# Joining the first loads to the list of steps, moving four x adds to GpSimd, and re-interleaving a tuned kernel

## The chip, the cores and the metric

The kernel runs on one core of a Trainium2 chip. The metric is the time of one execution in microseconds (us), measured on the device; each kernel is executed several times and the median is quoted. The profile's "span" is a little shorter than this time: it runs from the first to the last recorded piece of work. Each execution also gives the mean clock that TensorE was granted (1.0 is full, 0.5 is half).

## The reference

Linear attention over 8 batches, 8 heads, 576 positions and 64 features a head, followed by a gated layer over 4608 tokens of 512 features.

```python
q_s = softmax(q, axis=-1)                 # over the 64 features
k_s = softmax(k, axis=2)                  # over the 576 positions
kv  = einsum('bhsd,bhse->bhde', k_s, v)   # "key-value product"
x   = einsum('bhsd,bhde->bhse', q_s, kv)  # then laid out as (4608, 512)
H   = maximum(x @ w_h, 0)
T   = 1 / (1 + exp(-(x @ w_t + b_t)))
out = T * H + (1 - T) * x
```

## The kernel before

Each engine works through its own list in order, as the traces show: in the kernel before, the scale of batch 1's last q block starts at 32.28 us, behind a cast that waited for its data until 31.65. The kernel is a set of small step functions and one long list `order` that says in which order they are issued, so the list is the schedule of all engines. A step's name tells its engine: `exp_half` and `tanh` run on ScalarE; `q_sums`, `kv_norm`, `diff` and `blend` on VectorE; `q_scale_p`, `cast_v` and `add_x` on GpSimd; `kv_half`, `q_trans`, `x_pair`, `gate` and `carry` on TensorE. The parts that the change and the argument touch:

```python
def q_scale_p(b, n0, n1):                 # GpSimd: q exponentials times 1/sum
    e, r = eq[b][:, n0:n1], qsum[b][:, n0:n1]
    nc.gpsimd.tensor_mul(e, e, r.broadcast_to(list(e.shape)))

def gate(c, ob, ps=None):                 # TensorE: x @ w_t, four 128x512 matmuls ("pt")
    ...
def carry(c, ob):                         # TensorE: x @ (w_h - 1), the same shape ("ph")
    ...

# which 128-wide blocks of x are added on GpSimd, by pair of batches; TensorE adds the others
added = lambda g: ((0, 1), (0, 1), (0, 1), (0, 1, 2, 3))[g]

def add_x(c, ob):
    xv, gv = views(c)
    eng = nc.vector if (c, ob) == (B - 1, 3) else nc.gpsimd
    eng.tensor_add(gv(ob), gv(ob), xv(ob))

def turn_block(t, k_, xs, us):            # TensorE: turn a block to rows ("nat"), add x on the way
    dst = t[:, k_, :]
    if xs is not None:
        mm(dst, xs, ident, True, False)   # one more matmul where GpSimd has not added x
    mm(dst, us, ident, xs is None, True)

def warm_up(n):                           # TensorE: matmuls whose result nobody reads;
    for _ in range(n):                    # put in to keep the clock up (measured under a_fill)
        mm(warm, ident, wide, True, True)
```

q of batches 6 and 7 is turned by a DMA (`q_turn`, the tile `qsD`) instead of by TensorE. The loads of batches 0 and 1 and of the weights stand in front of the list, before any step.

The softmax here doesn't subtract the row's maximum and nothing guards it: scores larger than these inputs give would overflow.

## Time and profile before

| | before |
|---|---|
| time, median (lowest to highest of the first runs) | 129.05 us (128.37 to 129.15) |
| time, span and mean clock of the profiled run | 130.35 us (a slow run, over 1.5% above the fastest), 127.4 us, 0.962 |
| TensorE, VectorE, ScalarE, GpSimd busy | 88%, 76%, 73%, 59% |
| first gate group of batch 0 / key-value product of batch 1 / first gate group of batch 1 | 18.1 / 28.5 / 33.2 us |
| last row tile of the output starts (its last wait is on VectorE) | 123.2 us |

The page divides the span into 40 slices of 3.18 us; a digit is the busy share in tenths, and the PEclk row gives TensorE's clock in tenths of full. The lines themselves are shown in the prediction. Two groups matter for the adds: the x adds on GpSimd and the matmuls that turn blocks to rows. The columns are line, engine, operation, tiles, count, then busy us and mean ns of one, then the idle time before them. The first line is of the page, the second of the full list of groups (`--lines`); it holds the matmuls that add x:

```profile
L428 POOL TENSOR_TENSOR g<-g,xT 128x512 f16<-128x512 f16 x19 | 21.7, 1153 | 10.3 <-DVE g L417 9.5
...
L64 PE MATMUL nat<-ident,xT 128*128 128x128 f16 x48 | 7.9, 219 | 0.0
```

### The profile page before, as it was taken

The numbers are of one execution on the slowest core, as the hardware profiler recorded it, in microseconds if no ns is written. First come the engines' busy times: TensorE is split into PE (matmuls) and PEld (weight loads), VectorE is DVE, ScalarE is ACT, GpSimd is POOL, SyncE is SP. The second block draws the span as 40 slices with busy tenths as digits, with TensorE's granted clock in tenths as the row PEclk, the third lists the DMA queues.
The fourth block names the chain that finished last, engine by engine and source line by source line (L and its number), as shares of the span: only waits on it lengthen the run. The fifth ranks groups of instructions, "written<-read, shape, count | busy, mean of one in ns | idle before, by whom it ended". The sixth has DMA issues, their size and how long they took to land.

```text
span 127.4 us, 3361 instructions
## 1 busy us (share of the span) xinstructions
PE 111.8 (88%) x1375; PEld 62.1 (49%) x1375; DVE 96.2 (76%) x179; ACT 93.0 (73%) x130; POOL 75.0 (59%) x71
## 2 busy tenths in 40 slices
PE   4996599584699998999999998999999999999940
PEld 2343334252224643654564466555555555599820
DVE  1089548399938899899799997879975649799960
ACT  4156076995694879768997989999999794576740
POOL 2004524960679393996991697499797224855510
PEclk9999999999558999999999999999999999999995
DMA  3999999999999999999999999948517816007994
GB/s 127 349 377 388 404 404 408 413 410 413 403 413 410 413 400 413 410 406 408 418 412 412 404 412 413 390 108 226 211 26 141 342 49 291 5 39 332 422 380 150
DMA packets 20583, 41.24 MB, mean 324 GB/s; under 512 B 5460, under 2 KB 5976, under 8 KB 19544
## 3 DMA queue, kind: packets, MB, share of 16 engines
q1 hardware_dynamic: 20568, 41.03, 84.4%
q8 instruction: 10, 0.16, 0.5%
q14 instruction: 5, 0.04, 0.1%
HBM read 30.41 MB, written 9.44 MB: 313 GB/s over the span
## 4 chain that ended last, share of the span: by engine, by line
PE 54%; DMA 20%; DVE 11%; SPq 4%; ACT 4%; issue 2%; POOL 2%; DVEq 1%; POOLq 1%
PE ph L64 20%; PE pt L64 20%; DMA v<-in_v_dram 10%; DMA w32h<-in_moe_w_h_dram 10%; PE nat L64 7%; SPq L94 4%; DVE g L417 3%; PE pq L69 3%; PE px L64 2%; DVE r L228 2%; ACT pt L396 1%; DVE qsT L278 1%; PE psk L64 1%; DVE dd L409 1%; DVE kvn L217 1%
## 5 line engine op out<-in xcount | busy, mean ns | idle before, releaser
L258 POOL TENSOR_TENSOR eq<-eq,r 128x1024 f16<-128x1024 f16 (+2 forms) x16 | 29.7, 1878 | 12.0 <-DVE r L246 9.7
L64 PE MATMUL ph<-xT,w16h 128*128 128x512 f16 x128 | 33.7, 389 | 2.2 <-ACT w16h L114 1.6
L64 PE MATMUL pt<-xT,w16t 128*128 128x512 f16 x128 | 33.6, 395 | 0.0
L396 ACT ACTIVATE pt<-pt,bt 128x512 f32<-128x512 f32 (+1 forms) x40 | 24.5, 622 | 8.8 <-PE pt L64 8.6
L409 DVE SCALAR_TENSOR_TENSOR dd<-xT,ph 128x512 f16<-128x512 f16 x32 | 21.5, 678 | 10.9 <-PE ph L64 9.8
L428 POOL TENSOR_TENSOR g<-g,xT 128x512 f16<-128x512 f16 x19 | 21.7, 1153 | 10.3 <-DVE g L417 9.5
L417 DVE SCALAR_TENSOR_TENSOR g<-pt,dd 128x512 f16<-128x512 f32 (+1 forms) x40 | 24.7, 627 | 2.3 <-ACT pt L396 1.1
L178 ACT ACTIVATE eq<-q 128x1152 f16<-128x1152 f32 x16 | 18.4, 1165 | 5.7 <-DMA q<-in_q_dram 5.7
L64 PEld LDWEIGHTS <-w16t 128*128 128x128 f16 x160 | 15.1, 100 | 13.8 <-issue 2.8
L64 PEld LDWEIGHTS <-w16h 128*128 128x128 f16 x160 | 14.4, 99 | 14.7 <-issue 2.5
L178 ACT ACTIVATE ek<-k 128x1152 f16<-128x1152 f32 x16 | 18.7, 1172 | 1.8 <-DMA k<-in_k_dram 1.8
L228 DVE TENSOR_REDUCE r<-eq 128x18 f32<-128x1152 f16 x12 | 16.0, 1344 | 5.2 <-ACT eq L178 5.2
L468 ACT COPY o<-nat 128x512 f32<-128x512 f32 x28 | 16.6, 592 | 4.5 <-PE nat L64 4.0
L189 POOL CAST v<-v 128x1152 f16<-128x1152 f32 x12 | 13.9, 1184 | 9.8 <-DMA v<-in_v_dram 9.8
L64 PE MATMUL nat<-ident,g 128*128 128x128 f16 x142 | 16.3, 220 | 0.1
L64 PEld LDWEIGHTS <-g 128*128 128x128 f16 x144 | 12.4, 98 | 6.5 <-DVE g L417 1.1
L64 PE MATMUL warm<-wide,ident 128*128 128x512 f16 x41 | 11.0, 423 | 1.8 <-DVE wide L149 1.8
L278 DVE COPY qsT<-pq 128x1024 f16<-128x1024 f16 (+1 forms) x18 | 9.9, 552 | 2.2 <-PE pq L69 2.0
L69 PE MATMUL pq<-ident,eq 128*128 128x128 f16 x108 | 8.9, 221 | 3.0 <-POOL eq L258 1.8
L361 ACT CAST xT<-px 128x1024 f16<-128x1024 f32 x10 | 10.2, 1018 | 1.8 <-PE px L64 1.5
L69 PEld LDWEIGHTS <-eq 128*128 128x128 f16 x108 | 6.9, 98 | 6.1 <-POOL eq L258 2.1
L64 PEld LDWEIGHTS <-ident 128*128 128x128 f16 x46 | 4.7, 105 | 7.6 <-issue 2.3
(53 smaller groups left out, 105.3 us busy)
## 6 DMA issues: line engine op xcount, KB each, us to landing
out_dram<-o SPq DMA_DIRECT2D x8, 1024.0 KB, 4.6
q<-in_q_dram SPq DMA_DIRECT2D x7, 1152.0 KB, 13.4
k<-in_k_dram SPq DMA_DIRECT2D x7, 1152.0 KB, 12.9
v<-in_v_dram SPq DMA_DIRECT2D x5, 1152.0 KB, 14.6
v<-in_v_dram SPq DMA_DIRECT2D x6, 576.0 KB, 12.0
q<-in_q_dram SPq DMA_DIRECT2D x2, 576.0 KB, 4.1
k<-in_k_dram SPq DMA_DIRECT2D x2, 576.0 KB, 7.0
w32t<-in_moe_w_t_dram SPq DMA_DIRECT2D x1, 1024.0 KB, 10.9
```

Of the source, the lines that this page charges most:

```text
L64: mm = lambda o, l, r, st, sp: nc.tensor.matmul(o, l, r, start=st, stop=sp, skip_group_check=True)
L69: nc.tensor.matmul(o, i, ident, is_transpose=True, start=True, stop=True, skip_group_check=True,)
L178: nc.scalar.activation(dst[b][:, :, 2 * a : 2 * a + 2, :], in32[which][b][:, 2 * a : 2 * a + 2].rearrange("p c n d -> p n c d"), AF.Exp,)
L189: nc.gpsimd.tensor_copy(o, i)
L228: nc.vector.reduce_sum(qsum[b][:, :, h], eq[b][:, :, h, :], axis=AX.X)
L258: nc.gpsimd.tensor_mul(e, e, r.broadcast_to(list(e.shape)))
L278: nc.vector.tensor_copy(qsT[b][:, :, n0:n1, :], turned_q.pop((b, g)))
L396: nc.scalar.activation(ps, ps, AF.Tanh, bias=bt2[:, ob : ob + 1], scale=0.5)
L409: nc.vector.scalar_tensor_tensor(dd, xv(ob), -0.5, ps, op0=ALU.mult, op1=ALU.max)
L417: nc.vector.scalar_tensor_tensor(gv(ob), th, 1.0, dd, op0=ALU.add, op1=ALU.mult)
L428: eng.tensor_add(gv(ob), gv(ob), xv(ob))
L468: copy(rows_of_four((g, n // 4))[:, n % 4, :], nat.pop((g, n)))
```

## The change

It has three parts. The first loads become steps of the list, in a new order. Pairs 1 and 2 (chunks 2 to 5) get their third block of x added on GpSimd, so that TensorE saves 16 matmuls. And the whole list is interleaved anew, with the aim of leaving TensorE no stretch so thin that its clock is lowered. The diff is 26 KB, nearly all of it the list; its core:

```diff
-    for w in "qkv":
-        load(0, w, 2)
-    nc.sync.dma_start(brow, moe_b_t.rearrange("(k p) -> k p", p=P))
-    load_weight("t", moe_w_t, "q32")
-    load(1, "q")
-    load_weight("h", moe_w_h, "k32", 4)
-    load(1, "k")
-    load(1, "v", 2)
+    def load_bias():
+        nc.sync.dma_start(brow, moe_b_t.rearrange("(k p) -> k p", p=P))
@@
-    added = lambda g: ((0, 1), (0, 1), (0, 1), (0, 1, 2, 3))[g]
+    added = lambda g: ((0, 1), (0, 1, 2), (0, 1, 2), (0, 1, 2, 3))[g]
@@  (the list; the stretch around batch 1's last q block, before)
-        ("exp_half", 2, "q", 0), ("blend", 0, 0), ("exp_half", 2, "q", 1), ("kv_norm", 1),
-        ("x_pair", 1, 0, False, ("ht", "ht")), ("blend", 0, 1), ("x_copy", 1, 0, "AV"),
-        ("cast_v_head", 2, 0, "P"), ("x_pair", 1, 1, False, ("ht", "q2")),
-        ("q_sums_tree", 2, 0), ("x_copy", 1, 1, "AV"), ("q_scale_p", 1, 8, 9),
-        ("q_trans", 1, 2), ("gate", 0, 3, "nat"), ("cast_v_head", 2, 3, "A"),
@@  (the list; its start, and the same stretch, after)
+        ("warm_up", 24), ("load", 0, "q", 2), ("exp_half", 0, "q", 0), ("load", 1, "q"),
+        ("load", 0, "v", 2), ("cast_v", 0, 1), ("warm_up", 6), ("exp_half", 0, "q", 1),
+        ("warm_up", 1), ("q_sums", 0, 1), ("load", 0, "k", 2), ("warm_up", 4),
+        ...
+        ("blend", 0, 0), ("kv_norm", 1), ("q_scale_p", 1, 8, 9), ("q_trans", 1, 2),
+        ("x_pair", 1, 0, False, ("ht", "ht")), ("tanh", 0, 3), ("exp_half", 2, "q", 0),
+        ("q_copy", 1, 2), ("blend", 0, 1), ("x_pair", 1, 1, False, ("ht", "q2")),
+        ("cast_v_head", 2, 2, "P"), ("x_copy", 1, 0, "AV"), ("x_copy", 1, 1, "AV"),
+        ("gate", 1, 1), ("exp_half", 2, "q", 1), ("add_x", 0, 0), ("carry", 1, 2),
+        ...
```

## The prediction

The phase is where the clock's windows of 3.41 us begin. "0.50 and 1.00 only" is the granted clock of the kernel before, and "there" in "1153 ns there" is GpSimd.

> **What bounds the kernel now.** I read the page first, then windows cut at the clock's own steps, then the timeline and the chain of waits around the first idle stretch. Parts 1 and 2 of the page:
>
> ```profile
> PE 111.8 (88%) x1375; PEld 62.1 (49%) x1375; DVE 96.2 (76%) x179; ACT 93.0 (73%) x130; POOL 75.0 (59%) x71
> ...
> PE   4996599584699998999999998999999999999940
> ...
> PEclk9999999999558999999999999999999999999995
> DMA  3999999999999999999999999948517816007994
> ```
>
> One slice is 127.4 / 40 = 3.18 us. TensorE (PE) is the fullest engine and is nearly solid from slice 12 to the end. Before that it has holes, and there the DMA row is solid: the first 30 us run at the pace of the loads, the rest at the pace of TensorE. Loads keep the DMA row full to slice 26 (83 us), but from 33 us no compute engine shows a wait on a load, so they run ahead. In slices 11 and 12 TensorE's granted clock is half. Windows of the clock's length, 3.41 us (columns: window, length, busy us and count of PE, PEld, DVE, ACT, POOL; then granted clock, DMA share, GB/s):
>
> ```profile
> 21.98:25.39 3.41, 1.85 (x11) 0.76 (x10) 1.50 (x5) 3.31 (x6) 3.20 (x4) 1.00 1.04 410
> 28.81:32.22 3.41, 1.43 (x78) 0.74 (x66) 3.34 (x8) 2.10 (x2) 0.57 (x1) 1.00 1.04 411
> 33.00:35.63 2.63, 2.62 (x8) 1.11 (x9) 2.53 (x7) 1.36 (x3) 1.06 (x1) 0.50 1.04 405
> 35.63:39.05 3.42, 3.42 (x16) 1.09 (x15) 0.95 (x2) 3.42 (x5) 3.29 (x3) 0.50 1.04 411
> 39.05:42.46 3.41, 3.41 (x57) 1.93 (x56) 2.90 (x7) 1.50 (x4) 2.75 (x3) 1.00 1.04 411
> ```
>
> TensorE was busy 42% of 28.81 to 32.22, and the clock halved at 32.22. It was busy 54% of 21.98 to 25.39, and nothing happened. After the drop came a window 77% busy (nothing from 32.22 to 33.00, then 2.62 of 3.41 us), which did not bring the clock back; the next, full one did, at 39.05. So 33.00 to 39.05, 6.05 us of dense matmuls, ran at half speed and lost 3.0 us. What emptied 28.81 to 32.22, from the chain of waits cut to 28 to 36 us and the timeline of ScalarE:
>
> ```profile
> 18.78 12.73 DMA v<-in_v_dram
> ...
> 31.65 0.67 POOL v L197
> 32.32 0.64 POOL eq L258
> ...
> 33.01 0.40 PE pq L69 x2
> ```
> ```profile
> 30.12 2.22 ACT L178 ACTIVATE eq<-q 128x1152 f16<-128x1152 f32 x2 [1.41 <-DMA q<-in_q_dram]
> ```
>
> GpSimd (POOL) stands in its in-order list on a cast of batch 2's v, which lands at 31.65; the scale of batch 1's last q block stands behind it, and TensorE's transposes behind that. ScalarE (ACT) meanwhile waits for batch 2's q (30.12) and does two exponentials before the copy that frees x of batch 1.
>
> [...] 0.50 and 1.00 only, steps 3.41 us apart; whether the phase moves the drop, one profile cannot show. [...] 128x512 adds take 1153 ns there against 880 ns for the single one on VectorE (DVE). [...] the trace moves 403 to 413 in most slices to 80 us. So reordering loads cannot bring the same bytes sooner, only other bytes first.
>
> **The change part by part.**
>
> *First loads.* Before: q0, k0, v0, bias, gate weights, q1, carry weights, k1, v1. After: q0, q1, v0, k0, bias, gate weights, carry weights, k1, v1. At 2.9 us per 1.18 MB tensor (1.18 MB / 0.408 MB per us), k0 goes from second to fourth place and lands near 15.6 us instead of 9.8; q1 lands near 9.8 instead of 18.1. The same bytes precede v1, so v1 lands near 27.3 in both (GpSimd waits for it until 27.31 before). Batch 0's first gate moves from 18.1 us to about 20.8: two exponentials at 1.15 us after k0, 72 small matmuls 0.8, normalise 0.7, x 0.8, copies 1.5, weight casts to 20.7. That costs nothing: before batch 1's key-value product (28.47 before) stand four gate groups and three carry groups in the new order, three and four in the old. Seven groups at 0.86 us (the chain's length for four 512-wide matmuls) plus transposes are 6.9 us, and 20.8 + 6.9 = 27.7. The new order fills this stretch with real work late instead of real work early and warm-up later; counts of warm-up matmuls are equal (41 + 5).
>
> *The idle stretch.* In the new order batch 1's last q block is scaled before any cast of batch 2's v, so the wait to 33.0 falls. What remains: ScalarE has one exponential of batch 2's q ahead of the x copies. q2 has the same bytes before it, so 30.1 + 1.15 + 2 copies at 0.6 = 32.45 for the next gate group against 33.09 (33.01 and two small transposes). Gain 0.6 us. From 29.1 to 32.45 TensorE has about 1.0 us of work, so the clock may well fall here again in spite of the change's aim. But then solid work starts at 32.45, the window 32.22 to 35.63 would be 93% busy (the initial window, 1.50 to 4.91, was 91% busy and released the clock), and one half-clock window instead of two would be spent: gain 1.4 us. If it does not fall at all: 3.0 us. I weigh them 60 to 40: 2.0 us.
>
> *x adds.* Pairs 1 and 2 (chunks 2 to 5) get their third block's x added on GpSimd: 4 more adds at 1.15 us = 4.6 us of GpSimd. Taken away: 8 row tiles x 2 pairs = 16 matmuls of 128x128 with their weight loads (TensorE's list goes from 2751 rows to 2719). A tile of six of these takes 0.34 us in the chain, 57 ns each: 16 x 57 = 0.9 us, on the engine that bounds.
>
> *The rest of the interleaving* changes no counts. TensorE idles some 1.3 us between 40 and 121 us before; I see as many new small holes as closed ones (a gap of some 0.9 us near 44 us, where ScalarE does batch 3's exponentials, landing 38.9, ahead of a tanh and two x copies). I put 0. From the start of the last gate's matmuls (120.69) to the end, 6.7 us: same parts in almost the same order, 0.
>
> Sum: 0.6 + 2.0 + 0.9 = 3.5 us, all after 30 us, where TensorE's list sets the pace, so it should reach the end: 129.05 - 3.5 = 125.5 us.
>
> **The rivals.**
> 1. *GpSimd becomes the bound late.* After batch 7's q scales come five adds in a row (5.8 us). Counting back from the new end, TensorE reaches the first row tile of pair 2 near 95.8 us; the scales can end near 89.8 (before: 91.97 + 4.19 = 96.2), so the fifth add ends near 95.6. That is level; a slip costs 1 to 2 us, making 127. For it: the adds also wait for blends. Against: GpSimd is only 59% busy.
> 2. *The clock was not the loss in the timed runs.* [...] if the three timed runs had no drop, only 0.6 + 0.9 is left and the time is 127.5. For it: the profiled run, at 130.35 us, was 1.3 us slower than the median. Against: the three agree within 0.8 us, where a mixture would spread by 3.
> 3. *In-order waits on loads.* ScalarE now has exponentials of batches 3 and 4 right behind their loads (k4 near 50.3 us) and ahead of tanhs; late loads would starve the accumulators: 1 to 3 us, 127 to 128. Against: before, no wait on a load is left after 33 us, and the loads gain on TensorE with each batch (three tensors at 2.9 us per batch against 10 to 11 us of TensorE).
> 4. *It all works*: the clock never falls and small holes close: 129.05 - 0.6 - 3.0 - 0.9 - 1.0 = 123.5.
>
> **Range and chances.** The lower end is rival 4 with some tenths more; the upper is rivals 2 or 3 with a small slip. 2% faster means below 126.47, which the middle passes by 1 us; rivals 1 to 3 each take it above. Predicted 125.5 us, 123.0 to 128.0; faster 0.66, same 0.31, slower 0.03.
>
> **What would show it.** In the changed profile: first gate group near 20.8 us; batch 1's key-value product near 28.5; no wait of the q transposes on GpSimd at 33; dense gate groups from 32.5; PEclk with one or no slice of 5 near slice 11; row-tile matmuls fewer by 16 and x adds 23 on GpSimd; TensorE solid from 33 us. It would be wrong if the clock stays low for two windows or falls at a new place, if TensorE waits for x adds near 95 us, or if ScalarE's waits for loads of batches 3 and 4 exceed 1 us each.

What the traces show of four things that it leans on:

- Half clock is about half speed: in the kernel before eight gate matmuls of the same shape take 3.62 us from 33.19 at a granted clock of 0.50, and 1.89 us from 39.73 at 1.00.
- "Released the clock" is read from the pace of the first warm-up matmuls, as the granted clock reads 1.00 there throughout. In the kernel before 8 fall in 1.50 to 4.91 (91% busy) and 18 in the window after; in the changed kernel 10 in 3.60 to 7.02 (100% busy) and 18 in the next.
- That reordering brings the same bytes no sooner is inference from the 403 to 413 GB/s. The casts of batch 1's v, which wait for its load, start at 27.31 us before and at 27.10 after.
- The phase differs from profile to profile: in the eight of 14 in which the clock fell, the falls and rises within one profile are whole windows of 3.41 us apart, and counted back from them the first window begins 0.2 to 3.1 us after the span's start.

## The result, and the profile after

The changed kernel took 126.79 us (median of four runs, 126.67 to 126.93) against 129.0 us (128.37 to 129.15, four runs). The ratio is 0.984, 95% interval 0.980 to 0.987: 1.6% faster, which counts as "within 2%". Ratios in this document are the mean time of one kernel's fast runs over that of the other's fast runs of the same rounds, so they are not quite the ratio of the medians quoted. The time lies within the predicted range of 123.0 to 128.0, 1.3 us above its middle, and the class is the one given 0.31, not the one given 0.66.

Parts 1 and 2 of the page of the changed kernel; a slice is 124.9 / 40 = 3.12 us:

```profile
PE 110.9 (89%) x1359; PEld 61.0 (49%) x1359; DVE 94.5 (76%) x179; ACT 92.4 (74%) x130; POOL 78.9 (63%) x75
...
PE   4999757999586998999999999999998999999950
...
PEclk9999975699999999999999999999999999999997
```

The PEclk row still has its trough. It has moved from slices 11 and 12 to slices 6 to 8. Windows of the clock's length show why (the columns are those explained in the prediction):

```profile
13.85:17.26 3.41, 1.55 (x86) 1.26 (x83) 3.04 (x7) 2.33 (x2) 1.27 (x2) 1.00 1.05 408
17.26:20.68 3.42, 2.62 (x35) 0.71 (x23) 2.48 (x8) 0.78 (x2) 1.58 (x4) 0.50 1.06 405
20.68:24.09 3.41, 2.96 (x13) 1.21 (x11) 1.16 (x5) 2.86 (x6) 3.41 (x6) 0.50 1.04 409
```

TensorE was busy 45% of 13.85 to 17.26, and the clock fell at 17.26. It came back at 24.09, after a window 87% busy. This is the stretch of batch 0's key-value product, which in the new order comes with little else for TensorE to do.

The stretch that the change was aimed at, 28 to 38 us, is better in its first half. Its chain of waits, and the lines of TensorE, VectorE and GpSimd in order of time (start, length, then what):

```profile
30.49 0.68 DVE g L413
...
32.51 1.19 DVE xT L361 x2
33.70 1.28 DVE t L235
...
37.34 0.59 DVE dd L405
```
```profile
33.14 1.08 PE L64 MATMUL pt<-xT,w16t 128*128 128x512 f16 x4 [0.74 <-DVE xT L361]
...
37.98 1.02 PE L64 MATMUL pt<-xT,w16t 128*128 128x512 f16 x4 [0.88 <-DVE dd L405]
```
```profile
33.62 1.35 DVE L235 TENSOR_TENSOR t<-eq 128x576 f16<-128x576 f16 x1
...
36.06 0.45 DVE L235 TENSOR_TENSOR t<-eq 128x576 f16<-128x576 f16 x1
```
```profile
33.50 1.15 POOL L424 TENSOR_TENSOR g<-g,xT 128x512 f16<-128x512 f16 x1
```

The wait of the q transposes on GpSimd at 33 us is gone, as intended. But batch 1's first gate group starts at 33.14 us, where before it started at 33.19, since everything before it runs later by the clock lost at 17 us. Then comes a new hole: VectorE's sum of batch 2's q takes 1.35 us instead of the 0.45 us that the same instruction takes at 36.06. It starts while GpSimd's x add (33.50 to 34.65) is running and ends 0.32 us after it. It is not only in these lines: in the 20 cases of all runs in which such a sum starts beside a GpSimd instruction with 0.18 us or more still to run, it ends 0.31 to 0.32 us after that instruction (in the kernel before, for one, at 34.38 us, where GpSimd's add ends at 34.06). What makes it wait, the traces do not show. In a second trace of the changed kernel (the control of the last batch) the sum starts 0.02 us before the add; there it takes its 0.45 us, the add 1.43 instead of 1.15, and VectorE's next sum 1.14 instead of 0.31. VectorE's `diff` comes late by this, and TensorE waits 0.88 us for the accumulator bank that it frees.

Later, at batch 7's turned q, the chain of waits reads:

```profile
87.16 4.20 POOL eq L254 x2
...
91.38 4.89 DMA qsD<-eq
...
96.31 0.22 PE px_l L64 x2
```

TensorE waits for the transposed q here (0.50 us), where it did not before. GpSimd's x adds and the matmuls that add x on TensorE, to be held against those of before:

```profile
L424 POOL TENSOR_TENSOR g<-g,xT 128x512 f16<-128x512 f16 x23 | 26.1, 1154 | 6.3 <-DVE g L413 6.3
...
L64 PE MATMUL nat<-ident,xT 128*128 128x128 f16 x32 | 6.1, 219 | 0.0
```

GpSimd has its four adds more, and TensorE 16 of these matmuls fewer (48 to 32). Their row fell by 1.8 us, but matmuls overlap in the records (one of these is recorded with 219 ns, six in a row take 0.34 us in the chain of waits): TensorE as a whole is busy 0.9 us less.

Put together by milestones:

| | before | after | difference |
|---|---|---|---|
| first gate group of batch 0 | 18.11 | 22.24 | +4.1 |
| key-value product of batch 1 | 28.47 | 30.19 | +1.7 |
| first gate group of batch 1 | 33.19 | 33.14 | 0 |
| from there to the last row tile's last wait (123.18, 120.67) | 89.99 | 87.53 | −2.5 |
| from there to the end | 4.2 | 4.2 | 0 |

In the last long stretch the kernel before spent 33.19 to 39.05 at half clock, 5.86 us, which cost half of that, 2.93 us (by the 3.62 against 1.89 us for eight gate matmuls given above). So by this estimate it would have needed 87.06 us there without the drop. The changed kernel needs 87.53 us with 16 matmuls fewer. On this account the whole gain of the profiled pair is the clock drop that left this dense stretch; what the fewer matmuls gave, the new holes took. One run below bears it out as far as TensorE goes: the kernel before with nothing but its clock kept (two 32-bit matmuls) has its last wait at 120.63 us, 2.55 us earlier, where the whole change gives 2.51. In time that version gained nothing, because its last outputs landed late. And of the 2.2 us between the medians, 0.3 us lie outside the span (time minus span, 2.1 against 1.8 us); no run shows what they are.

### The profile page after: what moved, and what is told of

Read it like the earlier page. It is cut to its first block, busy times and chain, and to the rows that moved or that the text cites. A ratio compares the mean times of both kernels' runs of the same rounds, so it can differ in the third digit from the quotient of the medians.

```text
span 124.9 us, 3329 instructions
## 1 busy us (share of the span) xinstructions
PE 110.9 (89%) x1359; PEld 61.0 (49%) x1359; DVE 94.5 (76%) x179; ACT 92.4 (74%) x130; POOL 78.9 (63%) x75
## 4 chain that ended last, share of the span: by engine, by line
PE 51%; DVE 23%; POOL 11%; issue 4%; DMA 4%; ACT 3%; DVEq 1%; POOLq 0%; ACTq 0%
PE pt L64 17%; PE ph L64 13%; PE warm L64 9%; POOL eq L254 8%; PE nat L64 5%; DVE dd L405 5%; DMA qsD<-eq 4%; DVE qsT L274 3%; DVE r L224 3%; PE pq L69 3%; DVE t L235 2%; PE px L64 2%; DVE g L413 2%; DVE xT L361 2%; POOL v L185 1%
## 5 line engine op out<-in xcount | busy, mean ns | idle before, releaser
L64 PE MATMUL pt<-xT,w16t 128*128 128x512 f16 x128 | 33.0, 388 | 2.2 <-DVE xT L361 1.0
L64 PE MATMUL ph<-xT,w16h 128*128 128x512 f16 x128 | 32.1, 379 | 0.0
L424 POOL TENSOR_TENSOR g<-g,xT 128x512 f16<-128x512 f16 x23 | 26.1, 1154 | 6.3 <-DVE g L413 6.3
L64 PE MATMUL nat<-ident,g 128*128 128x128 f16 x142 | 14.6, 220 | 0.0
L64 PE MATMUL warm<-wide,ident 128*128 128x512 f16 x41 | 12.8, 477 | 1.8 <-DVE wide L144 1.8
L64 PEld LDWEIGHTS <-g 128*128 128x128 f16 x144 | 11.3, 98 | 5.4 <-DVE g L413 0.9
```

The costliest lines, as they stand in the source:

```text
L64: mm = lambda o, l, r, st, sp: nc.tensor.matmul(o, l, r, start=st, stop=sp, skip_group_check=True)
```

## The experiments

All ran in three batches of four kernels, each batch on a chip of its own, with the kernel before on the same chip, five rounds each. The kernel before varied: over its 33 runs on the three chips its span was 125.1 to 128.8 us. Of the 14 runs at a mean clock of 0.98 or above, 13 had spans of 125.1 to 126.1 us; the 19 at 0.955 to 0.978 had 126.0 to 128.8. One window of 3.41 us at half clock lowers the mean by about 3.41 / 127 / 2 = 1.3%, so the drop seems to be whole in some of its runs and shorter or absent in others. Its two runs at 0.992 had 125.1 and 125.3 us, within 0.4 us of the changed kernel's first four (124.9 to 125.1, with their own drop).

### Does the lost clock at 17 us explain the missing start gain?

Eleven warm-up matmuls put into the holes of 14 to 19 us of the changed kernel:

```diff
-        ("exp_half", 0, "k", 1), ("load", 1, "v", 2), ("kv_half", 0, 0), ("q_recip", 1),
-        ("q_copy", 0, 2), ("kv_half", 0, 1), ...
-        ("kv_norm", 0), ("warm_up", 2), ...
+        ("warm_up", 4), ("exp_half", 0, "k", 1), ("load", 1, "v", 2), ("kv_half", 0, 0), ("q_recip", 1),
+        ("warm_up", 4), ("q_copy", 0, 2), ("kv_half", 0, 1), ...
+        ("kv_norm", 0), ("warm_up", 5), ...
```

> The changed kernel with 11 more warm-up matmuls in the holes of 14.6 to 19.2 us (4 before each half of batch 0's key-value product, 3 more after it), nothing else. Theory: the half clock of 17.3 to 24.1 us in the changed kernel delays batch 0's first gates (12 matmuls in 3.46 us instead of 2.6) and with them batch 1's key-value product, from some 28.5 to 30.2 us; with the clock kept, the product starts near 28.8 and the first gate group of batch 1 near 32.5 instead of 33.1, so 0.6 us less: 126.2 us. Rival: from 28 us the loads (v1 27.3, q2 30.1) and VectorE's x copies set the pace and nothing changes: 126.8.

Measured: 126.36 us median (124.91 to 127.62), ratio 0.972 (0.965 to 0.979). The PEclk row of its profile shows no trough:

```profile
PE   4999797996888989988999999999999999999950
...
PEclk9999999999999999999999999999999999999996
```

Batch 0's first gate starts at 20.94 us (predicted 20.8), batch 1's key-value product at 27.97 (28.5), batch 1's first gate at 31.19 (32.45), and the span is 123.1 us, 1.8 us less. The first twelve gate matmuls take 2.75 us here and 3.67 us in the changed kernel. So the start would have been as predicted or better with the clock up; in this pair of profiles the drop cost 1.8 us, not 0.6. The median gains less than the profile, because three of the six runs were slow (two at 125.7 us of span with a clock of 0.984, one at 124.4 with full clock). Why those were slow was not settled.

### Is the clock alone worth something in the kernel before?

The same on the kernel before: three warm-up matmuls behind batch 1's key-value product and eight before its last q transposes.

```diff
@@  (warm_mid also takes a bank of a new name at each call)
-        ... ("kv_half", 1, 0), ("kv_half", 1, 1),
+        ... ("kv_half", 1, 0), ("kv_half", 1, 1), ("warm_mid", 3),
-        ... ("q_scale_p", 1, 8, 9),
+        ... ("q_scale_p", 1, 8, 9), ("warm_mid", 8),
```

> The kernel before with 11 more warm-up matmuls in the two holes of 29.4 to 33.0 us (3 after batch 1's key-value product, 8 after its x product), nothing else. Theory: the drop of the clock at 32.2 us is what the changed kernel mostly gains, so this kernel at full clock through 33 to 39 us falls by 2.5 to 3.0 us, to 126.0 to 126.5, below the changed kernel. Rival: other engines and loads (k2 lands at 36) would have held TensorE anyway in 33 to 39 us: less than 1 us, 128 or more.

Measured: 129.46 us (129.22 to 130.36), ratio 1.006 (1.001 to 1.011): nothing gained, where the theory had 126.0 to 126.5. Yet the profile shows full clock throughout, and batch 2's key-value product comes 3.0 us earlier (39.05 against 42.0). The gain is lost in two places. First, at batch 7's turned q, whose chain of waits reads:

```profile
89.14 4.19 POOL eq L261 x2
...
93.36 4.94 DMA qsD<-eq
...
98.34 0.22 PE px_l L64 x2
```

TensorE stands still for 1.13 us until the transpose lands; its last wait is then only 1.6 us earlier than before (121.55 against 123.18). Second, the last outputs land at 125.53 us, just when they did before (125.52). What holds them is taken up under "What holds the last outputs?" below.

### What are the four adds worth?

Taken out of the changed kernel (the 16 matmuls come back):

```diff
-    added = lambda g: ((0, 1), (0, 1, 2), (0, 1, 2), (0, 1, 2, 3))[g]
+    added = lambda g: ((0, 1), (0, 1), (0, 1), (0, 1, 2, 3))[g]
-        ("add_x", 2, 2),   ... ("add_x", 3, 2),   ... ("add_x", 4, 2),   ... ("add_x", 5, 2),
```

> The changed kernel without the four added x adds; the 16 transposing matmuls are back. Theory: 0.9 us of TensorE's time at 57 ns each comes back, minus up to 0.5 that the wait for batch 7's turned q near 96 us gives back as GpSimd is 4.6 us less loaded: 127.2 to 127.7. Rival: GpSimd's adds delay the q scales so much (chain 83.8 to 96.3 us) that leaving them out wins or is level: 126.3 to 126.8.

Measured: 127.46 us (126.58 to 128.21), ratio 0.989 (0.983 to 0.995), 0.6 to 0.7 us above the changed kernel. But TensorE's last wait came only 0.28 us later (120.95 against 120.67), and the 0.50 us wait at batch 7's turned q was gone. Those 0.28 us were there at batch 1's first gate already (33.43 against 33.14): from there to the last wait the two need 87.52 and 87.53 us. The rest is again behind the last matmul.

And the adds alone, put into the kernel before behind the steps that they need:

```diff
-    added = lambda g: ((0, 1), (0, 1), (0, 1), (0, 1, 2, 3))[g]
+    added = lambda g: ((0, 1), (0, 1, 2), (0, 1, 2), (0, 1, 2, 3))[g]
+        ("add_x", 3, 0), ("add_x", 2, 2), ...  ("add_x", 3, 1), ("add_x", 3, 2), ...
+        ("add_x", 5, 1), ("add_x", 4, 2), ...  ("blend", 5, 2), ("add_x", 5, 2), ...
```

> The kernel before with only the four x adds of the third block added to GpSimd's list, two behind the other adds of chunk 3, two behind those of chunk 5. Theory: 16 matmuls less on the engine that bounds, minus 0.9 us: 128.1. Rival: the adds push batch 7's q scales (92 to 96 us) back by 1.2 to 2.3 us and row tiles wait for them: 129.0 or more.

Measured: 132.55 us (132.28 to 133.81), ratio 1.030 (1.025 to 1.036): slower. TensorE's timeline and the chain of waits where it loses:

```profile
97.94 0.23 PE L64 MATMUL nat<-ident,g 128*128 128x128 f16 x1 [2.90 <-POOL g L428]
```
```profile
91.51 4.19 POOL eq L258 x2
95.70 1.09 POOL v L189
96.78 1.11 POOL g L428
```

The row tile waits 2.90 us for an add that stands in GpSimd's list behind the scales of batch 7's q and a cast, and TensorE's clock falls for one more window (98.5 to 101.9). This is the prediction's first rival, at the place it named and larger than the 1 to 2 us that it gave. In the order of the changed kernel no row tile waits for an add there.

### What holds the last outputs?

In the trace of every kernel there are transfers on queues marked "instruction", here called instruction fetches. Ten or so are of 16 KB (queue q8), each one packet of 0.9 to 1.5 us; a few are of 8 KB (q14). The transfers of the last microseconds, without the adds (118 to 127 us) and in the changed kernel (118 to 125 us); the columns of the outputs are size and us to landing:

```profile
q8 instruction: 1, 0.02, 1.1%
...
out_dram<-o SPq DMA_DIRECT2D x1, 128.0 KB, 3.6
```
```profile
q14 instruction: 1, 0.01, 0.5%
...
out_dram<-o SPq DMA_DIRECT2D x1, 128.0 KB, 2.4
```

Without the adds a 16 KB fetch falls at 120.5 us, among the last outputs, and the last of these takes 3.6 us; in the changed kernel the last such fetch is at 109.5 us, and it takes 2.4. In the same view the rates without the adds fall from some 350 to 390 GB/s to between 20 and 27 for the last 1.1 us, about a sixteenth. The page counts 16 DMA engines, so the reading was that one of them is held back; no trace here shows the engines one by one. To test this, seven more warm-up matmuls were added to the version with eleven, only to make TensorE's list longer:

```diff
-        ("warm_up", 4), ("q_copy", 0, 2), ...  ("kv_norm", 0), ("warm_up", 5), ...
+        ("warm_up", 6), ("q_copy", 0, 2), ...  ("kv_norm", 0), ("warm_up", 6), ...
-        ("x_pair", 1, 1, False, ("ht", "q2")),
+        ("x_pair", 1, 1, False, ("ht", "q2")), ("warm_mid", 4, 1),
```

> The changed kernel with the 11 warm-up matmuls of a_fill and 7 more (2 and 1 in the same holes, 4 in the hole of 30.2 to 31.2 us behind batch 1's x product), so that TensorE's list has 2755 rows; a_fill's has 2741, a_noadd's 2751. Theory: a 16 KB instruction fetch now falls among the last outputs, as in a_noadd (at 120.5 us) and b_fill (at 121.6 us), [...] and the last output lands 1.2 to 1.6 us later after its issue (3.2 us in those two, 2.1 in the changed kernel and in a_fill), though TensorE ends no later than in a_fill: 1.0 to 1.6 us slower than a_fill, near 126.4. Rival: the fetch is an accident of those two runs; a_rows is level with a_fill or 0.3 us faster as its clock is safer: 124.9 to 125.3.

Measured: 126.75 us (125.92 to 129.04), ratio 0.980 (0.974 to 0.987). TensorE's last wait ends at 118.81 us, as with eleven (118.88). A fetch now falls at 118.4 us, and the last data land at 122.77 instead of 121.77: 1.0 us, at the low end of what was expected. Two of the six runs were slow; the fast ones average 126.37 us, 1.15 above the fast ones with eleven (on another chip).

In the kernel before, the filling was repeated with two 32-bit matmuls, to lengthen the list as little as possible:

```diff
+    wide32 = consts.tile([P, 512], FP32, name="wide32")
+    nc.gpsimd.memset(wide32, 0.0)
-        ... ("q_scale_p", 1, 8, 9),
+        ... ("q_scale_p", 1, 8, 9), ("warm_32", 2, 1),      # mm(t, wide32[:, 0:128], wide32)
```

> The kernel before with the hole of 31.2 to 33.0 us filled by two float32 matmuls of 128x512 ([...] two rows of TensorE's list) instead of the 11 float16 ones of b_fill (22 rows). Theory: b_fill won 3.0 us from the kept clock up to 76 us (its gate groups run that much earlier), lost 1.1 of it to the wait for batch 7's turned q at 97 us and the rest to the instruction fetch among the last outputs; with hardly any rows added the fetch is gone and 1.4 to 1.6 us remain: span 125.5, time 127.6. Rival: the clock's gain is lost before the tail in any case: 128.6 or more.

A length of the 32-bit matmuls that no run had shown is cut from this expectation; in this run's trace the two take 1.98 us together (from 31.27 us).

Measured: 128.62 us (128.35 to 130.27), ratio 1.002 (0.995 to 1.008): a miss. TensorE's last wait was 2.55 us earlier than before, as its timeline shows:

```profile
120.63 0.23 PE L64 MATMUL nat_l<-ident,g 128*128 128x128 f16 x1 [0.93 <-DVE g L424]
```

But a fetch still fell at 120.3 us, and the last data landed at 124.39, only 1.1 us earlier; two of the six runs had a clock of 0.970 in spite of the filling. Over all 14 profiles the pattern holds: the last 128 KB output takes 3.4 to 3.6 us with a 16 KB fetch beside it (four kernels) and 1.9 to 2.7 us without (ten). Of these ten, the seven with an 8 KB fetch beside it have 2.4 to 2.7, and the three without one 1.9; as the seven are all versions of the changed kernel, this was not tested apart. What decides where a fetch falls was not found: a list of 2751 rows has one in the tail in the new order without the adds, and none in the kernel before.

### One swap in the kernel before

Only the scale of batch 1's last q block goes ahead of the cast of batch 2's v:

```diff
-        ("cast_v_head", 2, 0, "P"), ("x_pair", 1, 1, False, ("ht", "q2")),
-        ("q_sums_tree", 2, 0), ("x_copy", 1, 1, "AV"), ("q_scale_p", 1, 8, 9),
+        ("q_scale_p", 1, 8, 9), ("cast_v_head", 2, 0, "P"), ("x_pair", 1, 1, False, ("ht", "q2")),
+        ("q_sums_tree", 2, 0), ("x_copy", 1, 1, "AV"),
```

> The kernel before with one swap: GpSimd scales batch 1's last q block before it casts batch 2's first v head, so the wait to 33.0 us for v falls away. Theory: the next wait takes its place (ScalarE's two exponentials of batch 2's q ahead of the x copies, which end at 33.3), the first gate group with the new x stays, only the one of chunk 0 moves into the hole, 0.9 us; that also fills the weak clock window, so 1 to 2.5 us less: 127 to 128. Rival: x copies and clock stay as they are: 128.8 or more.

Measured: 127.42 us (126.78 to 128.69), ratio 0.989 (0.982 to 0.995), with a clock of 0.99 or above in all six runs and a profiled span of 124.9 us, the changed kernel's own. TensorE's timeline shows the hole it leaves:

```profile
30.77 1.03 PE L64 MATMUL pt<-xT,w16t 128*128 128x512 f16 x4
32.41 1.16 PE L64 MATMUL pt<-xT,w16t 128*128 128x512 f16 x4 [0.61 <-ACT xT L365]
```

A waiting gate group now runs in the hole, and with the 0.61 us that are left of it the clock did not fall. A ratio of 0.989 against 0.984: in time this one swap gives about two thirds of what the whole change gives, with intervals that overlap, and on another chip. In the span the profiles are level; the difference is the 0.3 us by which time minus span is longer in the versions of the kernel before. TensorE's last wait (120.74 us) is level with that of the kernel before with its clock kept (120.63) and of the changed kernel (120.67).

### The holes after 33 us

The x add of pair 0's first block is moved from 33.5 us to behind two later adds:

```diff
-        ("gate", 1, 1), ("exp_half", 2, "q", 1), ("add_x", 0, 0), ("carry", 1, 2),
+        ("gate", 1, 1), ("exp_half", 2, "q", 1), ("carry", 1, 2),
-        ("add_x", 1, 0), ("add_x", 0, 1), ("x_left", 2), ("blend", 1, 3),
+        ("add_x", 1, 0), ("add_x", 0, 1), ("add_x", 0, 0), ("x_left", 2), ("blend", 1, 3),
```

> The changed kernel with one x add of chunk 0 on GpSimd moved from 33.5 us to behind the adds of 45.9 us. Theory: VectorE's adds of 16-bit pairs slow down beside GpSimd (1.35 us instead of 0.45 for the one that meets this add at 33.6); without it batch 2's sums end some 0.9 us earlier, the hole of TensorE at 37.1 to 38.0 shrinks to nothing, and the time falls by 0.6 to 0.9 us. Rival: the slow adds are not the cause or the gain is given back at the next hole (39.9, 46.7): within 0.3 us of the changed kernel.

Measured: 125.94 us (125.37 to 127.16), ratio 0.978 (0.972 to 0.984). From the x copies to the `diff`, VectorE's sums of batch 2's q take 0.6 us less (33.71 to 37.26 in the changed kernel, 32.96 to 35.93 here), and TensorE's hole shrinks from 0.88 to 0.31 us. Part of the difference in time is the clock, which was half for one window (20.16 to 23.57) in this profile and for two in the first one of the changed kernel. Against the second trace of the changed kernel (the control of the last batch, half clock for one window too) little is left for the moved add: the hole is 0.47 us there, and of the 0.8 us between the two at TensorE's last wait (119.40 against 120.18), 0.6 are there before the add, at batch 1's first gate (32.38 against 33.00). In this version the sum meets GpSimd's cast instead and still takes 0.77 us.

### Last batch: control, both repairs, the adds again, and the order of loads

The changed kernel itself, once more:

> The changed kernel itself, as the control on this chip. Expected as at first: 126.8 us, 0.984 of the time before, within 0.005. If its clock falls in some runs only, as the kernel before showed on two chips, the runs should spread by over 1 us with the lower granted clock in the longer ones; if the fall at 17 us belongs to the holes of the new start whatever the phase, all runs agree within 0.5 us as the first four did.

Measured: 126.79 us (126.01 to 126.96), ratio 0.983 (0.978 to 0.988), the first result over again. In all ten runs of the changed kernel the clock is 0.948 to 0.983: it falls in every run. In two of these six it is 0.98 and the span is 124.2 to 124.3 us (the profiled one has half clock for one window, 21.24 to 24.65); in the other four it is 0.948 to 0.970 and the span is 124.9 to 125.2. The two profiles have their clock windows 0.56 us apart (rises at 24.65 and 24.09 us), and the clock is half for one window in this one and for two, 17.26 to 24.09, in the first; so the phase seems to decide how long the drop lasts, and this is worth up to 0.8 us of span.

Both repairs, the eleven warm-up matmuls and the moved add, together:

> The changed kernel with both repairs: 11 more warm-up matmuls between 14 and 19 us, and the x add of pair 0's first block moved from 36 us to behind the two later adds. If the losses are those two (the clock at the start, 1.8 us of span; VectorE's additions beside GpSimd's add at 37 us, some 0.6), they should add up: fast runs near 124.5 us, 0.966 of the time before, 0.7 us under the run with the warm-up matmuls alone. Rival: the gap at 37 us is a wait that only moves to the next of VectorE's or GpSimd's instructions; then 125.2 us, as with the warm-up matmuls alone.

Measured: 125.64 us (125.0 to 126.48), ratio 0.976 (0.970 to 0.981); the mean of its fast runs is 125.70 us against 126.60 for the control on the same chip. This is the fastest median, 0.7% under the changed kernel. But it is not the 124.5 us expected; the rival's 125.2 is nearer. The two repairs do not add up: with the start 1.7 us earlier, the moved add is what TensorE waits for.

```profile
47.87 0.28 PE L64 MATMUL nat<-ident,g 128*128 128x128 f16 x2 [0.64 <-POOL g L424]
```

The changed kernel without the adds, with a shorter list (two 32-bit warm-up matmuls, which took 1.98 us in the kernel before with its clock kept, in place of eight 16-bit ones, where eight gate matmuls of that shape take 1.89; 2736 rows instead of 2751):

```diff
-        ("load", 0, "v", 2), ("cast_v", 0, 1), ("warm_up", 6), ("exp_half", 0, "q", 1),
-        ("warm_up", 1), ("q_sums", 0, 1), ("load", 0, "k", 2), ("warm_up", 4),
+        ("load", 0, "v", 2), ("cast_v", 0, 1), ("warm_32", 2), ("exp_half", 0, "q", 1),
+        ("warm_up", 1), ("q_sums", 0, 1), ("load", 0, "k", 2), ("warm_up", 2),
```

> The changed kernel without the four added x adds again, but with 8 early warm-up matmuls of 16-bit replaced by two of 32-bit that last about as long, so that TensorE's list is 2736 rows rather than 2751. If the 0.7 us that the version without the adds lost is mostly the instruction fetch that fell among its last outputs, and the 16 matmuls themselves are worth some 0.3 us, the fetch leaves the tail and the time is 126.4 us (126.0 to 126.8), at or below the changed kernel's. If the 16 matmuls are worth their predicted 0.9 us, the time stays near 127.5 us.

Measured: 127.15 us (126.4 to 127.62), ratio 0.985 (0.980 to 0.991). The fetch did leave the tail (the last one is at 108.2 us), and the last output lands sooner:

```profile
out_dram<-o SPq DMA_DIRECT2D x1, 128.0 KB, 2.7
```

The mean of its runs, 127.06 us, lies between the two expectations (126.4 and 127.5) and 0.46 us above the control's 126.60, with intervals of the ratios that overlap. In the profile its stretch from batch 1's first gate to TensorE's last wait is 87.05 us (34.18 to 121.23), against 87.18 (33.00 to 120.18) for the control: in that stretch the adds gain nothing. They are worth 0 to 0.5 us, and that the changed kernel has no 16 KB fetch among its last outputs is luck, as far as these runs tell.

The changed kernel with the old order of the first loads (batch 0's k second, batch 1's q behind the gate weights, its exponentials and sums moved back):

```diff
-        ("warm_up", 24), ("load", 0, "q", 2), ("exp_half", 0, "q", 0), ("load", 1, "q"),
+        ("warm_up", 24), ("load", 0, "q", 2), ("exp_half", 0, "q", 0), ("load", 0, "k", 2),
-        ("q_scale_v", 0, 4, 9), ("q_trans", 0, 1, "q2"), ("exp_half", 1, "q", 0),
+        ("q_scale_v", 0, 4, 9), ("q_trans", 0, 1, "q2"), ("load", 1, "q"),
+        (exponentials, sums and reciprocals of batch 1's q behind batch 0's x copies)
```

> The changed kernel with the old order of the first loads: batch 0's k second and batch 1's q after the gate weights, with batch 1's q exponentials and sums moved behind batch 0's x copies. The prediction gave the order of the loads 0 us, since the same gate and carry groups stand before batch 1's key-value product: then within 0.5 us of the changed kernel, with batch 0's first gate near 18.5 to 20.7 us instead of 22.2. Rival: the new order is what empties 14 to 19 us and drops the clock at 17; then this version keeps its clock over that stretch and is 1 to 2 us faster, or loses it later instead, near 28 us, where the kernel before lost it.

Measured: 126.17 us (125.11 to 127.18), ratio 0.975 (0.968 to 0.983). The mean of all six spans is 124.33 us, against 124.82 for the control: within 0.5 us, as the prediction had it. But two of the six count as slow; the fast ones average 125.64 us against 126.60, 1.0 us less, as the rival had it. Which of the two holds is not settled, as the runs differ in kind. Two keep their clock (0.99 and 1.0, span 123.3 us), one loses a window (0.98, 123.9 us) and three have 0.973 to 0.985 and 124.9 to 125.4 us. No run of the changed kernel kept it, so the new order of loads may well cost part of what the drop costs. Batch 0's first gate starts at 18.43 us in this version, as early as expected, but after one matmul it has to wait for a weight:

```profile
20.57 3.96 PE L64 MATMUL pt<-xT,w16t 128*128 128x512 f16 x11 [1.76 <-POOL w16t L117]
```

## Why the prediction was right or wrong

The number was in its range and its middle 1.3 us too low; the sum behind it was 0.6 + 2.0 + 0.9 + 0 = 3.5 us. Its terms were off in both directions (the 0.6 did not come, the clock gave 0.9 more than 2.0 in the profiled pair, the holes lost 1.8), so that it came so near is partly luck. By its steps:

1. **What bounds the kernel before.** Right. The idle stretch at 32 us, the cast in GpSimd's list and the clock that fell with it were the cost: the swap of one scale and one cast removed the drop in all six runs and gave 1.1% by itself.
2. **"First gate … about 20.8", gain 0.6 us at batch 1's first gate.** The step that failed. The predicted times hold or are beaten when the clock is up (20.94, 27.97 and 31.19 us with eleven more warm-up matmuls). The terms listed for 20.8 add up to 21.7; the number is about right because only one exponential follows the whole of k (k comes in two parts, and the first exponential runs on the first). But the prediction looked for thin windows only between 29 and 33 us. It noted that the new order does the real work late and that the counts of warm-up matmuls are equal, and did not ask where those warm-up matmuls stood: the holes of 14 to 19 us had two, and a window there was 45% busy. The gain was 0 in place of 0.6, and the drop cost 1.8 us of span in the profiled pair; the prediction had weighed a new drop only near 32 us, where it would have cost 1.6 us of the clock's gain.
3. **The idle stretch and the clock, 2.0 us.** The mechanism was right: the dense matmuls from 33 us run at full clock, and that is 2.9 us in the profiled pair, close to the 3.0 of the better branch. The weighing of 60 to 40 put the risk at the wrong place, though "falls at a new place" was listed among the things that would make it wrong. In the timed runs it is worth less than in the profiles, since a good part of the runs of before have no or half of the drop, and the profiled one was a slow run. The second rival was therefore partly true; "the three agree within 0.8 us, where a mixture would spread by 3" was too few runs to tell, as 33 runs spread by 3.7 us of span.
4. **The adds, 0.9 us.** Mis-sized: 0 to 0.5 us. The matmuls do leave, but TensorE then arrives at batch 7's turned q before it has landed (0.50 and 0.57 us of waiting in the two profiles of the changed kernel, 0 and 0.24 us in the two without the adds). The prediction had batch 7's scales on GpSimd end near 89.8 us; they ended at 91.36. So the engine that bounds gave its gain back at the next thing that was late. The first rival, GpSimd's late adds, did not come in the changed order, and came in full when the adds were put into the old order (+3.0%).
5. **"The rest of the interleaving … I put 0."** Wrong by the new holes. Holes of TensorE of 0.12 us and more between 33 and 121 us sum to 1.1 us before (0.49, 0.16, 0.12, 0.32) and to 2.9 us after (0.88, 0.45, 0.13, 0.28, 0.27, 0.15, 0.26, 0.50): 1.8 us. The largest is VectorE's sum waiting behind GpSimd's x add. In the version that moves that add the hole is 0.57 us smaller than in the first profile of the changed kernel, but only 0.16 smaller than in the second, and in another version 0.64 us open elsewhere; so what the holes cost in the end is not simply their sum.
6. **The third rival, waits on loads.** Not seen: no wait of ScalarE on a load after 33 us is among the holes.
7. **"880 ns for the single one on VectorE".** Misread. That add starts while a GpSimd add is running, which ends at 113.16 us, and ends 0.29 us after it, so it seems to wait for it; in the changed kernel the same add takes 0.42 us. GpSimd takes 2.7 times as long for it (1154 against 424 ns), not 1.3 times. The lines of before, then that of after:

```profile
110.89 2.27 POOL L428 TENSOR_TENSOR g<-g,xT 128x512 f16<-128x512 f16 x2 [0.56 <-DVE g L417]
112.57 0.88 DVE L428 TENSOR_TENSOR g<-g,xT 128x512 f16<-128x512 f16 x1
```
```profile
110.98 0.42 DVE L424 TENSOR_TENSOR g<-g,xT 128x512 f16<-128x512 f16 x1
```

For the profiled pair the stretch from batch 1's first gate on then reads: −2.9 (clock) − 0.9 (matmuls) + 1.8 (holes) = −2.0, measured −2.5; the 0.5 us left over were not assigned.

What stays open: the slow runs of the version with eleven warm-up matmuls, what decides where an instruction fetch falls, what the new order of loads costs, the 0.3 us outside the span, and 0.5 us of the sum.

## What to carry to other kernels

When work is moved to close one thin stretch of TensorE, look at every window of the clock's length (3.41 us in these traces) in the new order, the filled ones of the old order included: here the drop moved to another thin one. Before counting on a gain of the engine that bounds, find the next transfer or step that it will then reach too early (here a transposed q and the outputs). And test the smallest part of a large re-interleaving alone: here one exchange of two GpSimd steps gave about two thirds of it in time.

## What the traces of this case show of the hardware

- The clock of TensorE: in 14 profiles, of all windows aligned with the clock's steps and before the kernel's end, the nine behind which it fell were 17 to 48% busy, and none of 52% or more made it fall. It did not come back after windows of 77, 77, 86 and 87%, and did after 84 and 87% and after full ones. So in these runs a window need not be idle for the clock to fall: seven of the nine were 42 to 48% busy.
- Transfers on the instruction queues: they are of 16 KB, and some of 8 KB; whether an engine ever waited for one the traces do not show. A 16 KB one is a packet of 0.9 to 1.5 us, and with one among the last outputs the last of them takes 3.4 to 3.6 us to land (four profiles) instead of 1.9 to 2.7 (ten).
- Two-input work: a 128x512 add of 16-bit numbers takes 1154 ns on GpSimd and 424 ns on VectorE, 2.7 times.
- VectorE beside GpSimd: VectorE's 128x576 addition takes 0.45 us alone, and up to 1.35 us here when it starts beside a GpSimd instruction, ending 0.31 to 0.32 us after it. Beside a cast with one input it takes longer too (0.77 us in the version with the moved add).
